# Attention output in column halves moved inside SBUF, and first weights converted in halves between the first products

## The chip, the core and the metric

The kernel runs on one core of a Trainium2 chip. The metric is the time of one execution in microseconds of device time; the median of three runs is taken.

## What is computed

A gated linear attention (a state of 48 x 48 numbers per head that decays and takes in one outer product per token) is followed by a SwiGLU feed-forward block. Everything is float32, but the three weight matrices arrive as float64.

```python
batch, n_heads, seq, head_dim = (4, 8, 768, 48)
for t in range(S):
    state = f[:, :, t, :, None] * state + np.einsum('bhd,bhe->bhde', k[:, :, t], v[:, :, t])
    y[:, :, t] = np.einsum('bhd,bhde->bhe', q[:, :, t], state)      # f = sigmoid(f_logit)
x = y.transpose(0, 2, 1, 3).reshape(B * S, H * D)                   # 3072 tokens x 384
g = x @ w_gate; silu = g / (1 + exp(-g)); val = x @ w_val           # d_ff = 1536
out = (silu * val) @ w_out
```

## The kernel before, in words

The 768 steps are cut into six chunks of 128 tokens. A unit is one batch of one chunk; the order is chunk 0 with its four batches, then chunk 1, and so on. While the feed-forward block of chunk c runs for its 512 tokens, the attention of chunk c + 1 is dealt in between (`take_turns`, L1001, with four steps a unit from `attention_steps`, L618). The general path at the head of the file runs only if a gate underflows; it does not in these runs.

**Attention of a unit** (`attention`, L504). Scans of the forget gate give factors for k and q; heads lie in pairs, one head in partitions 0 to 47, its neighbour in 64 to 111. Eight products of 48 rows give the scores (L563, `sc`), VectorE masks them into `A` (L565), and for all but the last chunk k is turned back by TensorE (L570, `kt`). Then comes the output `y`, feature by token, in one PSUM bank. Its 384 features are cut into quarters of 32: `place(n)` (L581) puts quarter n into partition group n mod 4. So that x comes out with 128 features in 128 partitions, quarters of 32 cross the borders of the heads of 48. From chunk 1 on, twelve products with `blocks` add the part of the state (L587): `blocks` holds the decayed state of a head pair as a block diagonal, filled by two ScalarE copies (L549). Sixteen products with v and `A` add the part inside the chunk (L596). One ScalarE copy (L599) moves the bank into `xT[c]`, the input of the feed-forward block. Eight products (L603, `dS`) and one VectorE sum (L607) update the state.

**Feed-forward.** Chunk 0 uses plain products (`mlp_plain`, L649): 12 gate and 12 val tiles of three products each, then the output (L679). Chunks 1 to 5 (`mlp_fifteen`, L778) form a 3 x 3 by 3 x 2 block product with 15 products instead of 18, four times over: sums of token blocks first (`token_sums`, L784, tile `xs`), then products into PSUM banks A, B, o and c (L825), copied aside by ScalarE (L830), added by VectorE (L717, L720). The output product takes seven products instead of eight (`down_seven`, L901; L923 and L977). The sums of weight blocks that this needs (`weight_sums`, L736) are made once, on VectorE, late in chunk 0 and in chunk 1.

**Weights.** They are fetched as float64 in 18 pieces of 768 KB and made float32: two ScalarE passes over a piece (`sizes`, L455 and L457) and four VectorE passes (`join`, L463 to L467). A gate or val piece covers two tiles of 128 columns. In `weights` (L1012) one fetch, one `sizes` and one `join` are dealt out after every pair of tiles.

**What sets the order.** Loads are issued by SyncE in one queue. Up to the mark near L1067 the order on TensorE, VectorE and ScalarE is that in which the code is written (`in_order`, L627); after that the Tile framework's scheduler places instructions, and each engine then works through its list in that order. Until L1067 the code walks through the attention of chunk 0 batch by batch, converts two pieces, and starts the products afterwards. The pool of attention tiles has one buffer for each tile.

Of the kernel before, what the change touches and what calls it, by code (L numbers as in the profile page):

```python
# [289 lines left out]
def short_path(ctx, tc, ident, least, judge, q, k, v, f_logit, moe_w_gate, moe_w_val, moe_w_out, out):  # L290
# [81 lines left out]
    decayed = const.tile([128, HP, D], FP32, tag="decayed", name="decayed")  # L372

    blocks = const.tile([128, HP, 2 * D], FP32, tag="blocks", name="blocks")
    nc.gpsimd.memset(blocks, 0.0)

    vs = [(const if i < NV // 2 else first_pool).tile([128, H, W], FP32, tag=f"v{i}", name=f"v{i}")
          for i in range(NV)]
    for t in vs:
        nc.gpsimd.memset(t[:, :, D:W], 0.0)  # L380

    w_both = const.tile([128, 2, KT, DFF], FP32, tag="w_both", name="w_both")
# [50 lines left out]
    def weight_piece(dst, src):  # L433

        if src.dtype == FP32:
            return (lambda: nc.sync.dma_start(out=dst, in_=src)), (lambda: None), (lambda: None)  # L440
        shape = list(dst.shape)
        kept = {}

        def fetch():
            kept["w"] = wst.tile(shape[:2] + [2 * shape[2]], I32, tag="w64", name="w64", bufs=3)
            nc.sync.dma_start(out=kept["w"], in_=src)

        def halves():
            words = kept["w"].rearrange("p a (n two) -> p a n two", two=2)
            return words[:, :, :, 0], words[:, :, :, 1]  # L450

        def sizes():
            lo, hi = halves()
            up = wst.tile(shape, I32, tag="up", name="up")
            nc.scalar.activation(up, lo.bitcast(U32), AF.Copy, scale=2.0 ** -29)  # L455
            top = wst.tile(shape, I32, tag="top", name="top")
            nc.scalar.activation(top.bitcast(FP32), hi.bitcast(FP32), AF.Abs)  # L457
            kept["up"], kept["top"] = up, top

        def join():  # L460
            lo, hi = halves()
            up, top = kept["up"], kept["top"]
            nc.vector.tensor_scalar(top.bitcast(FP32), top.bitcast(FP32), as_float(0x38000000), as_float(0x47F00000),  # L463
                                    op0=ALU.max, op1=ALU.min)
            nc.vector.tensor_scalar(top, top, 3, 0x3FFFFFFF, op0=ALU.logical_shift_left, op1=ALU.bitwise_and)
            nc.vector.scalar_tensor_tensor(top, hi, -(1 << 30), top, op0=ALU.bitwise_and, op1=ALU.bitwise_or)
            nc.vector.tensor_tensor(dst.bitcast(I32), top, up, ALU.add)  # L467

        return fetch, sizes, join
# [10 lines left out]
    NW = 256  # L480

    def add_piece(dst, src):
        for group, f in zip((fetches, sizes, joins), weight_piece(dst, src)):
            group.append(f)

    for j in range(0, DFF, NW):
        for dst, src in ((w_gate, moe_w_gate), (w_val, moe_w_val)):
            add_piece(dst[:, :, j:j + NW], in_rows(src)[:, :, per * j:per * (j + NW)])
    for i in range(NF // 2):
        both = slice(i, NF, NF // 2)  # L490
        add_piece(w_out[:, both, :], in_rows(moe_w_out)[:, both, :])
# [12 lines left out]
    def attention(u):  # L504
# [40 lines left out]
        if c:  # L545
            nc.vector.tensor_tensor(decayed, states[b], whole.broadcast_to((128, HP, D)), ALU.mult)
            for par in range(2):
                r = rows_of(par)
                nc.scalar.copy(blocks[r, :, par * D:(par + 1) * D], decayed[r])  # L549
# [4 lines left out]
        if 0 < c < SQUARES:  # L554
            load_after(u)
# [19 lines left out]
        if b == 0:  # L575
            xT[c] = ffn.tile([128, KT, TB], FP32, tag="xT", name="xT", bufs=2)


        y = bank("y")

        def place(n):  # L581
            return y[Q * (n % 4):Q * (n % 4) + Q, n // 4 * C:(n // 4 + 1) * C]

        per = 2 * D // Q
        if c:
            for n in range(DM // Q):
                nc.tensor.matmul(place(n), lhsT=blocks[:, n // per, n % per * Q:(n % per + 1) * Q], rhs=qT[:, n // per, :],  # L587
                                 start=n < 4, stop=False, skip_group_check=True)
        flat = v_.rearrange("t h e -> t (h e)")
        met = {n % 4 for n in range(DM // Q)} if c else set()  # L590
        for par in range(2):
            for n in range(DM // Q):
                h = 2 * (n // per) + par
                at = n * Q - h * D
                if -Q < at < D:
                    nc.tensor.matmul(place(n), lhsT=flat[:, W * h + at:W * h + at + Q], rhs=A[:, par, n // per, :],  # L596
                                     start=n % 4 not in met, stop=par == 1 or at + Q <= D, skip_group_check=True)
                    met.add(n % 4)
        nc.scalar.copy(xT[c][:, :, b * C:(b + 1) * C], y[:, 0:DM].rearrange("p (a t) -> p a t", t=C))  # L599
        if c < NCH - 1:  # L600
            p = bank("dS")
            for h in range(H):
                nc.tensor.matmul(p[W * (h % 2):W * (h % 2) + W, (h // 2) * D:(h // 2 + 1) * D],  # L603
                                 lhsT=kt[:, h, :], rhs=v_[:, h, 0:D], start=True, stop=True)
            dS = p[:, 0:HP * D].rearrange("p (a d) -> p a d", d=D)
            if c:
                nc.vector.tensor_tensor(states[b], decayed, dS, ALU.add)  # L607
            else:
                nc.scalar.copy(states[b], dS)
# [39 lines left out]
    def mlp_plain(c):  # L649
        h = {}  # L650

        def product(w, j, name):
            p = fps.tile([128, 512], FP32, tag="m", name=name)[:, 0:TB]
            for i in range(KT):
                nc.tensor.matmul(p, lhsT=w[:, i, j * 128:(j + 1) * 128], rhs=xT[c][:, i, :],  # L655
                                 start=(i == 0), stop=(i == KT - 1))
            return p

        def part(j):
            if j % NP not in h:  # L660
                h[j % NP] = hidden_tile()
            k = 2 * (j // NP)
            return h[j % NP][:, k:k + 2, :].rearrange("p a t -> p (a t)")

        def gate(j):
            p = product(w_gate, j, "gate")
            nc.scalar.activation(part(j), p, AF.Silu)

        def val(j):
            p = product(w_val, j, "val")  # L670
            nc.vector.tensor_tensor(part(j), part(j), p, ALU.mult)

        return ([lambda j=j, f=f: f(j) for i in range(0, NF, 2) for f in (gate, val) for j in (i, i + 1)],
                downs_abreast(c, h))
# [50 lines left out]
    extra = sums_pool.tile([128, 6, 2, NG], FP32, tag="extra", name="extra")  # L725

    def every_second(t, odd):

        return t.rearrange("p g (n two r) -> p g n two r", two=2, r=128)[:, :, :, odd, :]

    def weight_parts():
        w = {(i, k): w_both[:, :, k, i * NG:(i + 1) * NG] for i in range(KT) for k in range(KT)}
        e = [extra[:, n] for n in range(6)]
        return w, e

    def weight_sums(odd):  # L736

        w, e = weight_parts()
        w = {n: every_second(t, odd) for n, t in w.items()}
        e = [every_second(t, odd) for t in e]  # L740
# [37 lines left out]
    def mlp_fifteen(c):  # L778
# [32 lines left out]
        def triple(j):  # L811
            cols = slice(j * 128, (j + 1) * 128)
# [6 lines left out]
            def product(r):  # L819
                name, a, b = PRODUCTS[r]  # L820
                fresh = name == "o" or name not in p
                if fresh:
                    p[name] = both(name)
                for n in range(2):
                    nc.tensor.matmul(p[name][:, n, :], lhsT=weights_of[a][:, n, cols], rhs=tokens[b],  # L825
                                     start=fresh and n == 0, stop=True, skip_group_check=True)
# [208 lines left out]
    def load_ahead(u):  # L1035

        if u + NRAW < B:
            load(u + NRAW, "fkq")
            load(u + 1, "v")
        elif u + 1 < B:  # L1040
            load(u + 1, "v")
        if u + 1 < B:
            fetches.pop(0)()
        if u + NRAW >= B:
            load(u + NRAW)
# [19 lines left out]
    sizes.pop(0)()  # L1065
    joins.pop(0)()
    in_order(mark, (mybir.EngineType.PE, mybir.EngineType.DVE, mybir.EngineType.Activation))  # L1067


    for c in range(NCH):  # L1070
        if c == 0:
            hidden, last = mlp_plain(c)

            hidden = [f for i in range(NF) for f in hidden[2 * i:2 * i + 2] + [weights]]
            for i in range(len(joins) - NF):
                last.insert(3 * i, weights)
# [8 lines left out]
        take_turns(pieces, attention_steps(c + 1) if c + 1 < NCH else [], 2 if c else 8)  # L1085
# [85 lines left out]
```

## Time and profile before

| what | value |
|---|---|
| median of 3 runs | 632.69 us (630.79 to 632.91) |
| profiled execution | 630.66 us, span 628.9 us, granted TensorE clock 1.00 |
| TensorE busy | 611.1 us, 97% of the span |
| VectorE, ScalarE busy | 497.9 us (79%), 297.4 us (47%) |
| DMA | 48.00 MB in all, mean 76 GB/s, 237 GB/s at most in a slice |

A float32 product shows as two LDWEIGHTS records (`PEld`) and two MATMUL records (`PE`). The ends of matmuls are modelled and overlap, so durations of neighbouring groups are compared by their starts. In brackets behind an instruction stands how long its engine was idle before it, and what ended that.

### The profile page before, as it was taken

The page shows a single profiled execution, that of the slowest core. Times are in us where ns is not written, and L with a number is a line of the kernel's source. Part 1 is how long each engine was busy: PE and PEld are TensorE (multiplying, and loading weights), DVE is VectorE, ACT ScalarE, POOL GpSimd, SP SyncE. Part 2 cuts the span into 40 slices and gives each one's busy share as a digit, 9 for nine tenths or more (in the row PEclk, how much of TensorE's full clock was granted, in tenths as well). Part 3 has the DMA queues.
Part 4 walks back from the last instruction along what each step waited for, and adds up shares of the span by engine and source line. Part 5 has one row for each costly group of instructions (what it writes and reads, how often), then busy time and mean ns, then how long its engine had stood idle before and what let it go on. Part 6 is the DMA issues. An engine that isn't in the chain of part 4 may idle for free.

```text
span 628.9 us, 11292 instructions
## 1 busy us (share of the span) xinstructions
PE 611.1 (97%) x4420; PEld 494.2 (79%) x4420; DVE 497.9 (79%) x941; ACT 297.4 (47%) x546; POOL 3.2 (1%) x22
## 2 busy tenths in 40 slices
PE   7899999999999999999999999999999999999996
PEld 4744555666877899888889888889988889988896
DVE  7887889968999997589897479987678994357641
ACT  2463657214667812667631556650365540166600
POOL 1000000000000000000000000000000000000000
PEclk9999999999999999999999999999999999999999
DMA  9997465024222204122213213322301200100001
GB/s 152 237 223 236 146 177 163 3 67 134 62 67 76 73 21 123 38 66 71 69 39 89 75 27 74 83 60 69 97 27 39 64 1 1 52 1 2 0 1 55
DMA packets 87517, 48.00 MB, mean 76 GB/s; under 512 B 53664, under 2 KB 81312, under 8 KB 87456
## 3 DMA queue, kind: packets, MB, share of 16 engines
q1 hardware_dynamic: 84144, 42.68, 28.6%
q10 hardware_dynamic: 3312, 4.52, 2.0%
q8 instruction: 36, 0.59, 0.4%
q14 instruction: 25, 0.20, 0.1%
HBM read 42.47 MB, written 4.72 MB: 75 GB/s over the span
## 4 chain that ended last, share of the span: by engine, by line
PE 80%; DVE 10%; DMA 4%; ACT 4%; issue 1%; SPq 0%; ACTq 0%; DVEq 0%
PE o L923 17%; PE A L825 13%; PE B L825 11%; PE o L679 5%; PE gate L655 5%; PE val L655 5%; PE o L825 4%; PE c L825 4%; PE sc L563 3%; PE o L977 3%; PE y L596 2%; PE y L587 2%; DVE c L720 2%; PE kt L570 1%; DVE h L842 1%
## 5 line engine op out<-in xcount | busy, mean ns | idle before, releaser
L923 PE MATMUL o<-w_out,h 128*128 128x192 f32 x360 | 62.5, 330 | 1.2 <-ACT c L940 0.7
L825 PE MATMUL A<-xs,w_both 128*128 128x256 f32 x240 | 62.0, 380 | 0.0
L923 PEld LDWEIGHTS o<-w_out,h 128*128 128x128 f32 x360 | 58.2, 190 | 3.0 <-ACT c L940 1.5
L717 DVE TENSOR_TENSOR c<-c,aside 128x512 f32<-128x512 f32 x60 | 41.7, 695 | 21.3 <-ACT aside L830 20.5
L830 ACT COPY c<-A 128x512 f32<-128x512 f32 x40 | 23.4, 586 | 61.7 <-PE A L825 61.6
L830 ACT COPY aside<-A 128x512 f32<-128x512 f32 x60 | 35.2, 586 | 32.3 <-PE A L825 32.2
L825 PEld LDWEIGHTS A<-xs,w_both 128*128 128x128 f32 x240 | 45.1, 190 | 6.2
L842 DVE TENSOR_TENSOR h<-h,c 128x256 f32<-128x256 f32 x100 | 41.8, 426 | 7.6 <-ACT h L841 7.6
L720 DVE TENSOR_TENSOR c<-c,aside 128x512 f32<-128x512 f32 x60 | 41.7, 696 | 2.1 <-ACT aside L830 1.8
L841 ACT ACTIVATE h<-c 128x256 f32<-128x256 f32 x100 | 41.8, 421 | 2.4 <-DVE c L717 1.2
L825 PE MATMUL A<-xs,extra 128*128 128x256 f32 x160 | 41.3, 380 | 1.6 <-ACT c L830 0.9
L825 PE MATMUL B<-xs,w_both 128*128 128x256 f32 x160 | 41.9, 384 | 0.2
L825 PE MATMUL B<-xT,extra 128*128 128x256 f32 x160 | 41.6, 382 | 0.0
L825 PE MATMUL c<-xT,w_both 128*128 128x256 f32 x160 | 41.3, 380 | 0.0
L923 PE MATMUL o<-ws,h 128*128 128x192 f32 x240 | 41.0, 327 | 0.0
L830 ACT COPY aside<-B 128x512 f32<-128x512 f32 x60 | 35.0, 584 | 9.9 <-PE B L825 9.6
L923 PEld LDWEIGHTS o<-ws,h 128*128 128x128 f32 x240 | 39.0, 190 | 0.2
L720 DVE TENSOR_TENSOR c<-o,c 128x512 f32<-128x512 f32 x40 | 28.1, 703 | 13.2 <-PE o L825 12.7
L563 PEld LDWEIGHTS sc<-qT,kT 48*128 48x128 f32 x384 | 25.7, 187 | 12.9 <-issue 9.4
L825 PEld LDWEIGHTS A<-xs,extra 128*128 128x128 f32 x160 | 30.2, 190 | 6.5 <-ACT c L830 1.3
L599 ACT COPY xT<-y 128x384 f32<-128x384 f32 x24 | 11.5, 477 | 49.8 <-PE y L596 49.8
L565 DVE TENSOR_TENSOR A<-sc,causal 128x512 f32<-128x512 f32 x48 | 31.1, 688 | 3.9 <-PE sc L563 3.9
(127 smaller groups left out, 1197.1 us busy)
## 6 DMA issues: line engine op xcount, KB each, us to landing
fsquares<-in_f_logit_dram SPq DMA_DIRECT2D x64, 96.0 KB, 2.3
ksquares<-in_k_dram SPq DMA_DIRECT2D x64, 96.0 KB, 2.3
qsquares<-in_q_dram SPq DMA_DIRECT2D x64, 96.0 KB, 2.4
v<-in_v_dram SPq DMA_DIRECT2D x24, 192.0 KB, 3.7
w<-in_moe_w_gate_dram SPq DMA_DIRECT2D x6, 768.0 KB, 6.5
w<-in_moe_w_val_dram SPq DMA_DIRECT2D x6, 768.0 KB, 5.9
w<-in_moe_w_out_dram SPq DMA_DIRECT2D x6, 768.0 KB, 4.5
out_dram<-ob ACTq DMA_DIRECT2D x23, 192.0 KB, 1.9
```

Source lines behind the costliest of these rows:

```text
L563: nc.tensor.matmul(sc[par][:, a * C:(a + 1) * C], lhsT=kT[r, a, :], rhs=qT[r, a, :], start=True, stop=True)
L565: nc.vector.tensor_tensor(A[:, par], sc[par].rearrange("p (a t) -> p a t", t=C), causal.unsqueeze(1).broadcast_to((128, HP, C)), ALU.mult)
L655: nc.tensor.matmul(p, lhsT=w[:, i, j * 128:(j + 1) * 128], rhs=xT[c][:, i, :], start=(i == 0), stop=(i == KT - 1))
L679: nc.tensor.matmul(p, lhsT=h[n // 2][:, n % 2 * 2 + b // 2, b % 2 * C:(b % 2 + 1) * C], rhs=w_out[:, j, :], start=(n == 0), stop=(n == NF ...
L717: nc.vector.tensor_tensor(dst, a, b, ALU.add)
L720: nc.vector.tensor_tensor(dst, a, b, ALU.subtract)
L825: nc.tensor.matmul(p[name][:, n, :], lhsT=weights_of[a][:, n, cols], rhs=tokens[b], start=fresh and n == 0, stop=True, skip_group_check=True)
L830: nc.scalar.copy(t, p[name])
L841: nc.scalar.activation(dst, src[:, 0, :], AF.Silu)
L842: nc.vector.tensor_tensor(dst, dst, src[:, 1, :], ALU.mult)
L923: nc.tensor.matmul(p[:, n, :], lhsT=lhsTs[j][:, n * C:(n + 1) * C], rhs=rhs[:, j, :], start=first and j == 0 and n == 0, stop=j == NP - 1, ...
L977: nc.tensor.matmul(p3[:, n, :], lhsT=h[j][:, 2, n * C:(n + 1) * C], rhs=b22[:, j, :], start=n == 0 and j == 0, stop=j == NP - 1, skip_grou ...
```

## The change

It has three parts.

1. **Output in column halves.** Chunk 0 keeps the quarters of 32 columns (there is no state part yet). From chunk 1 on a head's 48 features, padded to 64, go to one half of the partitions, in two PSUM banks, one for each head of a pair: eight products with the decayed state (48 rows, 64 columns) and eight with v (128 rows, 64 columns). `blocks` and its two copies go; `decayed` gets padding columns that stay zero. Two ScalarE copies bring the banks to a tile `yT`, and ten DMA transfers from SBUF to SBUF, issued by SyncE, put the pieces of the heads (48, 32 or 16 partitions by 128 tokens) into their partitions of `xT[c]`.
2. **First weights in halves.** The pieces of the first two gate and the first two val tiles are converted in two halves each, in the order gate 0, val 0, gate 1, val 1, and the first products follow the conversions: gate 0, val 0, gate 1, val 1. The four products and the first two attention steps of chunk 1 now stand in the part whose order is written out. A fourth buffer holds fetched pieces, and the piece of val tiles 2 and 3 is fetched before the inputs of unit 5.
3. **Layout of the weights.** `w_both` holds the columns by tiles of 128 (`[128, 2, NF, KT, 128]`), so that a half is one run. One VectorE pass of a `join` becomes two over half the elements where a piece has two tiles.

```diff
-    w_both = const.tile([128, 2, KT, DFF], FP32, tag="w_both", name="w_both")
+    w_both = const.tile([128, 2, NF, KT, 128], FP32, tag="w_both", name="w_both")
...
-            kept["w"] = wst.tile(shape[:2] + [2 * shape[2]], I32, tag="w64", name="w64", bufs=3)
+            kept["w"] = wst.tile([128, a, 2 * b * n], I32, tag="w64", name="w64", bufs=4)
...
-            nc.vector.scalar_tensor_tensor(top, hi, -(1 << 30), top, op0=ALU.bitwise_and, op1=ALU.bitwise_or)
+            for i in range(b // parts):
+                nc.vector.scalar_tensor_tensor(top[:, i], hi[:, i], -(1 << 30), top[:, i], op0=ALU.bitwise_and,
+                                               op1=ALU.bitwise_or)
...
-            for par in range(2):
-                r = rows_of(par)
-                nc.scalar.copy(blocks[r, :, par * D:(par + 1) * D], decayed[r])
...
         if c:
-            for n in range(DM // Q):
-                nc.tensor.matmul(place(n), lhsT=blocks[:, n // per, n % per * Q:(n % per + 1) * Q], rhs=qT[:, n // per, :],
-                                 start=n < 4, stop=False, skip_group_check=True)
...
+            y = [bank("y") for _ in range(2)]
+            def place(a, par):
+                return y[par][W * (a % 2):W * (a % 2) + W, a // 2 * C:(a // 2 + 1) * C]
+            for a in range(HP):
+                for par in range(2):
+                    r = rows_of(par)
+                    nc.tensor.matmul(place(a, par), lhsT=decayed[r, a, :], rhs=qT[r, a, :],
+                                     start=a < 2, stop=False, skip_group_check=True)
+            for par in range(2):
+                for a in range(HP):
+                    nc.tensor.matmul(place(a, par), lhsT=v_[:, 2 * a + par, :], rhs=A[:, par, a, :],
+                                     start=False, stop=a >= HP - 2, skip_group_check=True)
+            yT = att.tile([128, 2, HP // 2 * C], FP32, tag="x", name="yT")
+            for par in range(2):
+                nc.scalar.copy(yT[:, par, :], y[par][:, 0:HP // 2 * C])
+            for h in range(H):
+                a, par = h // 2, h % 2
+                f = h * D
+                while f < (h + 1) * D:
+                    n = min((h + 1) * D, (f // 128 + 1) * 128) - f
+                    r = W * (a % 2) + f - h * D
+                    nc.sync.dma_start(out=xT[c][f % 128:f % 128 + n, f // 128, b * C:(b + 1) * C],
+                                      in_=yT[r:r + n, par, a // 2 * C:(a // 2 + 1) * C])
+                    f += n
...
     run(B - 1, 4)
-    sizes.pop(0)()
-    joins.pop(0)()
+    hidden, last = mlp_plain(0)
+    steps = attention_steps(1)
+    for _ in range(2):
+        sizes.pop(0)()
+        joins.pop(0)()
+    load(B + 1, "v")
+    for _ in range(2):
+        sizes.pop(0)()
+    hidden[0]()
+    joins.pop(0)()
+    steps.pop(0)()
+    joins.pop(0)()
+    hidden[1]()
+    weights()
+    hidden[2]()
+    steps.pop(0)()
     in_order(mark, (mybir.EngineType.PE, mybir.EngineType.DVE, mybir.EngineType.Activation))
```

## The prediction

> **What bounds the kernel now.** I read the page first, then busy time by stage, then the order of time around the places that the change touches.
>
> ```profile
> span 628.9 us, 11292 instructions
> PE 611.1 (97%) x4420; PEld 494.2 (79%) x4420; DVE 497.9 (79%) x941; ACT 297.4 (47%) x546; POOL 3.2 (1%) x22
> DMA  9997465024222204122213213322301200100001
> ```
>
> TensorE is busy nearly all the time; only the first eighth loads the DMA engines heavily. Busy time by stage (start; chunk 0; chunk 1; chunk 2):
>
> ```profile
> core 0: us, PE busy (x) PEld busy (x) DVE busy (x) ACT busy (x) POOL busy (x), PEclk, DMA share, GB/s
> 0.00:33.00 33.00, 26.45 (x341) 19.32 (x342) 27.42 (x49) 12.75 (x23) 2.91 (x19) 1.00 1.15 194
> 33.00:147.00 114.00, 114.00 (x649) 62.34 (x648) 95.94 (x161) 51.35 (x74) 0.24 (x3) 1.00 0.53 140
> 147.00:248.00 101.00, 96.86 (x765) 83.65 (x764) 98.34 (x184) 55.27 (x103) 0.00 (x0) 1.00 0.30 77
> 248.00:348.00 100.00, 99.18 (x777) 86.03 (x776) 80.97 (x158) 54.73 (x100) 0.00 (x0) 1.00 0.25 64
> ```
>
> After 33 us TensorE has no gap in chunk 0; in chunk 1 VectorE, at 98 of 101 us, is as full as TensorE. So a saving counts only where it shortens TensorE's work or the 33 us before the first product; in chunk 1 time that VectorE loses counts too. Scores and output of one unit in order of time on TensorE:
>
> ```profile
> 286.22 1.16 PE L563 MATMUL sc<-qT,kT 48*128 48x128 f32 x16
> 287.31 0.66 PE L570 MATMUL kt<-idf,kT 128*128 128x128 f32 x4
> ...
> 292.21 0.86 PE L587 MATMUL y<-qT,blocks 128*32 128x128 f32 x24
> 292.89 1.07 PE L596 MATMUL y<-A,v 128*32 128x128 f32 x32
> 293.90 0.67 PE L603 MATMUL dS<-v,kt 128*64 128x48 f32 x16
> 294.50 1.13 PE L825 MATMUL B<-xs,w_both 128*128 128x256 f32 x4
> ```
>
> The 24 records of the state part take 0.68 us from start to start: four run abreast, six rounds of 0.11 us. The next 32 are eight rounds, 0.88, and 0.13 more until `dS`, whose shape differs. `sc`, with two row halves abreast, has eight rounds in 1.09 us with its switch. The start of the products:
>
> ```profile
> 30.87 0.63 PE L513 MATMUL fTp<-idf,fraw 128*128 128x128 f32 x4 [0.36 <-DMA fraw<-in_f_logit_dram]
> 31.65 0.66 PE L513 MATMUL kTp<-idf,kraw 128*128 128x128 f32 x4 [0.15 <-DMA kraw<-in_k_dram]
> 32.76 0.63 PE L513 MATMUL qTp<-idf,qraw 128*128 128x128 f32 x4 [0.45 <-DMA qraw<-in_q_dram]
> 33.22 5.32 PE L655 MATMUL gate<-xT,w_both 128*128 128x512 f32 x12
> ```
>
> TensorE waits for the inputs of unit 4, though `xT` is complete at 30.46.
>
> **What the Trainium skill says.** "TensorEngine Tiling (Array Packing)", Key Properties: different tiles of the array run in parallel, and a change of tiling mode drains it. The trace agrees: rounds of four and of two, and 0.13 us at the switch. The same page, Gotcha 1: row tiles must write to different PSUM banks, hence two banks now, as `sc` has. "DMA: Bandwidth & Descriptors", Anatomy of one DMA: a semaphore wait is served on the issuing sequencer, before the transfer; so a transfer that waits for `yT` holds up the loads behind it. "TensorE: Matmul & The Clock Gate", on the array's sub-arrays: ScalarE and VectorE are strict FIFO; so a sum that waits for `xT` holds up every later VectorE instruction.
>
> **The change part by part.**
>
> *TensorE, output.* The twelve products with `blocks` become eight of 48 x 64. Two row halves by two column halves let four run abreast: four rounds instead of six. No row shows this tiling; bounds are four rounds (0.44) and, if only two run abreast, eight (0.88). I take four, because rows and columns each show it alone. The v part stays at eight rounds (16 records, two abreast). The switch moves: one between state part and v part, none before `dS`, which has the v part's shape. Balance: two rounds, 0.22 us a unit, in 16 units; in the last chunk's four, which have no `dS`, one switch is added: 0.22 - 0.13 = 0.09. The scheduled order breaks attention groups apart more often in chunks 1 and 4 (some five more pieces) and less often in chunk 2 (two fewer). A break costs two switches, some 0.3 us. Sum: chunk 0 stage -0.9; chunk 1 -0.9 + 1.0; chunk 2 -0.9 - 0.6; chunk 3 -0.9; chunk 4 -0.4 + 0.3.
>
> *ScalarE.* 40 copies of 348 ns go, 20 of 477 ns become 40 of half a bank (nearest row 421 ns, 256 elements): 23.4 us become 16.8. ScalarE is half idle, and waits of TensorE for it sum to some 4 us; I count nothing.
>
> *SyncE and xT.* 200 transfers of at most 24 KB. Issue: 0.34 us (an output's issue) to 0.43 (a square's, 1.73 us for four); landing 1.9 to 2.3 us. So `xT` is complete 0.85 + 3.4 to 4.3 + 2 = 6.3 to 7.2 us after the last product of `y`, against 0.5 before. Who waits: the token sums on VectorE, and behind them the evacuations of the output product. At the border of chunks 2 and 3 `y` ends at 337.8; `xT` at 344.8, ten sums at 0.335 and three evacuations make 349.5; TensorE wants the last of the first sums at 351.05. Hidden, with 1.5 us to spare. At the border of chunks 0 and 1 `y` ends at 133.3, `xT` comes at 140.3. VectorE has independent weight sums until 138.3, so it stands 2 us, and finishes the token sums at 144 instead of 141.6; several semaphores to wait for cost some more. Later VectorE is idle for 1.1 us before 151.43 and twice 0.25, which absorbs most; the rest, 0.8 us, comes out where L923 waits for VectorE's `h` at 221.12. The loads behind the transfers are needed a unit later: nothing. `yT` has one buffer, refilled 15 us later at the earliest: nothing.
>
> *Start.* Half a piece costs VectorE some 1.5 us instead of 3.0; `A` ends at 29.2, so gate 0 can start at 30.7, 2.5 us earlier. But 1.35 us of that was the work of the transposes of unit 4, which only move behind it: gain 1.1 us. Against it: the scan of unit 4 now stands behind the conversion of val tiles 2 and 3 and part of the next piece, whose transfer lands near 44.6 (ScalarE waited for it until 44.61). With 1.8 us of ScalarE and some 4 us of VectorE behind it, qT is ready near 50.6, and TensorE reaches `sc` at 49.5: it stands 1.1 us. I count -0.2.
>
> *Conversion in two passes of half size*: 12 extra passes, 0.06 us each on VectorE, beside TensorE's full 114 us: nothing. Layout: the products read as many rows as before: nothing.
>
> Sum: -0.2 - 0.9 + 0.8 (chunk 1: breaks and saving cancel, VectorE's delay stays) - 1.5 - 0.9 - 0.1 = -2.8; for the borders I add 0.3. 632.7 - 2.5 = 630.2 us.
>
> **Rivals.** *A clear gain* (chance 0.26): nothing of the transfers is seen, the start keeps its 1.1 us, ScalarE's relief takes 0.6 us of waits: 632.7 - 4.1 (0.22 x 16 + 0.09 x 4, with 0.2 of breaks) - 1.1 - 0.6, about 626.9. For it: TensorE's own work really shrinks, and 97% of the span is TensorE. Against: VectorE is full in chunk 1. *The transfers come too late* (0.18, slower): with other loads in the queue and eight transfers under way at a time, `xT` lands 10 us after `y`; VectorE then stands at all five borders, TensorE 1.5 to 2 us behind each, chunk 1 3 us: 632.7 - 3.5 + 8 = 637. For it: SyncE's squares at 0.43 us stand in the same queue. Against: 1.5 us to spare. *The small tiles do not run four abreast* (0.08, slower): eight rounds, 0.44 us x 20 more than forecast: 639. The forecast has 0.48.
>
> **How the numbers follow.** The likeliest case gives 630.2. A spread of 2 us (the three runs differ by that) puts 0.2 of its 0.48 below 629.5. With the rival's 0.24: faster 0.43. The two slow cases give 0.22 above 635.9; the rest is no change. From 625.8 to 637.0 holds 8 in 10.
>
> **What would show it.** Right: the state part at four rounds, 0.46 us between starts, and `y` to `dS` 1.47 us instead of 1.69; gate 0 near 30.7 with a wait at the first `sc` near 50; VectorE waiting about 2 us for the DMA of `xT` near 138, and no TensorE wait at later borders. Wrong: state-part records in pairs; issues of the transfers above 0.5 us, or sums that stand at every border; a longer stall near 50.

## The result, and the profile after

The changed kernel took 636.23 us (median of 4, 634.45 to 636.77) against 631.96 us of the kernel before beside it: ratio 1.0064, 95% interval 1.0034 to 1.0093. It is slower by some 4 us, where 2.5 us less was forecast. The time lies inside the range given, on the wrong side.

From the page of the profiled execution (634.45 us), the span, the busy times and the granted TensorE clock in 40 slices:

```profile
span 632.7 us, 10670 instructions
PE 610.4 (96%) x3940; PEld 492.4 (78%) x3940; DVE 501.3 (79%) x959; ACT 289.6 (46%) x530; POOL 2.9 (0%) x22
PEclk9999999999998999999999999999999999999999
```

TensorE has 480 records fewer and is busy for 0.7 us less, in a span that is 3.8 us longer. One slice has a lower clock; in the page of the kernel before every slice has 9. Busy time by stage (start; chunk 0; chunk 1; chunk 2):

```profile
core 0: us, PE busy (x) PEld busy (x) DVE busy (x) ACT busy (x) POOL busy (x), PEclk, DMA share, GB/s
0.00:31.00 31.00, 24.89 (x331) 18.22 (x331) 25.77 (x48) 10.27 (x20) 2.64 (x19) 1.00 1.15 193
31.00:147.00 116.00, 113.99 (x561) 62.80 (x562) 96.56 (x173) 55.26 (x77) 0.24 (x3) 1.00 0.54 146
147.00:251.60 104.60, 99.28 (x670) 84.91 (x669) 100.72 (x189) 54.48 (x99) 0.00 (x0) 0.98 0.30 77
251.60:350.00 98.40, 97.95 (x682) 85.30 (x682) 81.27 (x157) 48.64 (x93) 0.00 (x0) 1.00 0.30 78
```

The first product starts 2 us earlier, and chunk 0 takes 2 us more, so nothing is left of the start. Chunk 1 grows by 3.4 us and has a mean clock of 0.98; chunk 2 shrinks by 1.7 us. The output of one unit in order of time on TensorE (start, duration, line, tiles, count):

```profile
296.10 0.67 PE L600 MATMUL y<-qT,decayed 48*64 48x128 f32 x16
296.70 1.09 PE L604 MATMUL y<-A,v 128*64 128x128 f32 x16
297.62 0.62 PE L637 MATMUL dS<-v,kt 128*64 128x48 f32 x16
298.18 1.13 PE L855 MATMUL B<-xs,w_both 128*128 128x256 f32 x4
```

From `y` to `dS` it is 1.52 us (1.69 before), from `y` to the next product 2.08 us (2.29 before). The single records of the state part start in four groups of four. So TensorE does save 0.21 us a unit; in the four units of the last chunk it is 0.06 (1.62 us from `y` to the next product, 1.68 before). The start:

```profile
31.20 2.81 PE L689 MATMUL gate<-xT,w_both 128*128 128x512 f32 x6 [0.68 <-DVE w_both L473]
...
48.04 1.88 PE L689 MATMUL val<-xT,w_both 128*128 128x512 f32 x4
51.73 1.16 PE L574 MATMUL sc<-qT,kT 48*128 48x128 f32 x16 [1.81 <-DVE qT L562]
```

And what TensorE waited for in the whole execution (total us, times, longest), two lines of its waits, first changed, then before:

```profile
PE sc L574 <- DVE qT L562: 5.7, 5, 1.8
PE o L1007 <- DVE ob L752: 3.5, 4, 1.5
```

```profile
PE sc L563 <- DVE qT L553: 1.9, 3, 0.8
PE o L977 <- DVE ob L717: 0.4, 1, 0.4
```

`ob` holds the output on its way out: its instructions on VectorE are the evacuations of the output product. Together the two waits are 6.9 us more: more than the 3.6 us that the shorter output saves in 16 units at 0.21 and four at 0.06.

For what follows, the time from the first product of a chunk to that of the next (the last one to the end), in us from the traces. Three of them hold stretches in which TensorE ran at half its clock, each 1.7 us of the time given: one in chunk 1 of the changed kernel and of the one with evacuations first, one each in chunks 0 and 1 of the one without transfers. The section on the clock comes to them.

| kernel | first product | chunk 0 | 1 | 2 | 3 | 4 | 5 |
|---|---|---|---|---|---|---|---|
| before | 33.22 | 113.66 | 101.23 | 100.12 | 99.07 | 93.56 | 88.03 |
| changed | 31.20 | 115.78 | 104.62 | 98.39 | 98.95 | 94.22 | 89.57 |
| halves of the output alone | 33.41 | 112.51 | 102.99 | 98.38 | 97.65 | 94.59 | 89.16 |
| start and layout alone | 31.17 | 116.04 | 101.27 | 100.10 | 99.09 | 93.56 | 87.96 |
| order held, no transfers | 31.21 | 117.46 | 104.52 | 98.46 | 97.54 | 93.70 | 87.86 |
| order held, evacuations first | 31.21 | 115.78 | 104.60 | 97.80 | 97.48 | 93.87 | 88.03 |
| order mended, third | 31.10 | 113.90 | 103.07 | 97.80 | 97.55 | 94.06 | 88.18 |

### The profile page after: what moved, and what is told of

It is laid out like the page before. It is cut to its first block, busy times and chain, and to the rows that moved or that the text cites. A ratio compares the mean times of both kernels' runs of the same rounds, so it can differ in the third digit from the quotient of the medians.

```text
span 632.7 us, 10670 instructions
## 1 busy us (share of the span) xinstructions
PE 610.4 (96%) x3940; PEld 492.4 (78%) x3940; DVE 501.3 (79%) x959; ACT 289.6 (46%) x530; POOL 2.9 (0%) x22
## 4 chain that ended last, share of the span: by engine, by line
PE 70%; DVE 14%; ACT 4%; SPq 4%; DMA 4%; issue 3%; DVEq 0%; ACTq 0%
PE A L855 13%; PE o L953 13%; PE B L855 11%; PE o L855 4%; PE c L855 4%; PE val L689 4%; PE sc L574 4%; SPq L615 4%; PE gate L689 3%; PE o L714 3%; PE y L604 3%; PE o L1007 2%; PE y L600 2%; DMA xT<-yT 2%; PE kt L581 1%
## 5 line engine op out<-in xcount | busy, mean ns | idle before, releaser
L574 PE MATMUL sc<-qT,kT 48*128 48x128 f32 x384 | 30.3, 287 | 5.7 <-DVE qT L562 5.7
L855 PEld LDWEIGHTS B<-xT,extra 128*128 128x128 f32 x160 | 30.0, 191 | 6.6 <-ACT aside L860 2.4
L855 PEld LDWEIGHTS c<-xT,w_both 128*128 128x128 f32 x160 | 30.8, 193 | 4.2
```

The source lines that it names most:

```text
L574: nc.tensor.matmul(sc[par][:, a * C:(a + 1) * C], lhsT=kT[r, a, :], rhs=qT[r, a, :], start=True, stop=True)
```

## Which part of the change costs the time

**Theory T:** the transfers make `xT` late; the token sums stand, and what is behind them on VectorE and SyncE comes late. **Rival S:** the new order of the start costs more than it gains. First each part alone. The diffs from here on are shortened.

The kernel before with the output's part of the diff, and nothing of the start or the layout:

```diff
-        y = bank("y")
+            y = [bank("y") for _ in range(2)]
...
-        nc.scalar.copy(xT[c][:, :, b * C:(b + 1) * C], y[:, 0:DM].rearrange("p (a t) -> p a t", t=C))
+                    nc.sync.dma_start(out=xT[c][f % 128:f % 128 + n, f // 128, b * C:(b + 1) * C],
+                                      in_=yT[r:r + n, par, a // 2 * C:(a // 2 + 1) * C])
```

> The kernel before with only the output in halves and the SBUF transfers; first weights and layout as before. Theory T (the transfers make xT late, so token sums stand and the evacuations and loads behind them come late): nearly all of the 4 us loss is here, 635 to 637 us. Rival S (the new order of the start costs more than it gains): without it the halves keep their 0.2 us a unit, 628 to 630 us.

The other way round, the changed kernel with the output of before:

```diff
-            y = [bank("y") for _ in range(2)]
+            y = bank("y")
...
-                    nc.sync.dma_start(out=xT[c][f % 128:f % 128 + n, f // 128, b * C:(b + 1) * C],
+        nc.scalar.copy(xT[c][:, :, b * C:(b + 1) * C], y[:, 0:DM].rearrange("p (a t) -> p a t", t=C))
```

> The changed kernel with the output put back to quarters and one ScalarE copy; conversion of the first weights in halves, their order and the layout stay. Theory T: the same as before within 1 us, 631 to 633 us, because the earlier first product (2 us) is lost again at the first score product. Rival S: 635 to 637 us.

Halves alone: 631.63 us, ratio 1.0001 (0.9989 to 1.0013). Start alone: 631.40 us, 0.9998 (0.9985 to 1.0011). Neither theory had this: each part by itself costs nothing, and only both together cost 0.6%. S falls, since the start alone is free: its first product is 2.05 us earlier and its chunk 0 is 2.38 us longer. T is half right: with the halves alone the chunks differ from before by -1.15, +1.76, -1.74, -1.42, +1.03 and +1.13 us. The output saves what it should in chunks 0, 2 and 3, and chunks 1, 4 and 5 take it back. That the two together cost more than either shows in their waits: for the evacuation TensorE waits 2.3 us with the halves alone and 3.5 in the changed kernel, at the first score product 1.2 us with the start alone and 1.8 in the changed kernel. Much of the rest is clock, as will be seen.

Then the transfers. One kernel leaves them out (ScalarE copies the two banks straight into `xT`, where the features then stand in wrong rows), one issues half of them from ScalarE:

```diff
-            yT = att.tile([128, 2, HP // 2 * C], FP32, tag="x", name="yT")
+            to = xT[c][:, :, b * C:(b + 1) * C]
...
-                nc.scalar.copy(yT[:, par, :], y[par][:, 0:HP // 2 * C])
+            nc.scalar.copy(to[:, 0:2, :], y[0][:, 0:HP // 2 * C].rearrange("p (a t) -> p a t", t=C))
+            nc.scalar.copy(to[:, 1:3, :], y[1][:, 0:HP // 2 * C].rearrange("p (a t) -> p a t", t=C))
```

> The changed kernel with the 200 transfers left out: ScalarE copies the two banks of y straight into xT, 256 columns each, so the features of xT stand in the wrong rows and a third of them is overwritten. Theory T: the waits behind the late xT (3.8 us before the last output products, 3.4 us in chunk 1) go and the shorter y stays, 628 to 630 us. Rival S: 635 us. Rival W (the small tiles save nothing on TensorE): 632 us.

```diff
-                    nc.sync.dma_start(out=xT[c][f % 128:f % 128 + n, f // 128, b * C:(b + 1) * C],
+                    (nc.scalar if h % 2 else nc.sync).dma_start(out=xT[c][f % 128:f % 128 + n, f // 128, b * C:(b + 1) * C],
```

> The changed kernel with the transfers of the odd heads issued from ScalarE instead of SyncE, so that ten issues of 0.59 us become two lists of five and xT is complete some 3 us earlier. Theory T: about half of the loss is regained, 633 to 634.5 us. Rival S: 636 us. Rival C (ScalarE's own work is delayed by the issues): above 636 us.

Without transfers: 630.53 us, 0.9979 (0.9968 to 0.9989), less of a gain than T said. With two queues: 635.36 us, 1.0067 (1.0048 to 1.0087), nothing regained. There TensorE waits only 1.2 us before L1007 instead of 3.5, but 4.6 us for ScalarE's copies `aside` instead of 1.2: an issue holds ScalarE's queue for 0.60 us (median of 100), and the copies stand behind it. That is rival C of this expectation.

These four kernels share one weakness: the scheduler places instructions anew after every edit. Without the transfers it puts a score product elsewhere, and TensorE stands near 3 us for it in chunk 1 (2.80 by the profile), and the mean clock is 0.994. So the next kernels hold the order.

## The same with the order held

Each engine's list is kept as the changed kernel's program has it; `ORDER` holds the numbers of the instructions as the code writes them, in the order of that program.

```diff
+    for name, order in ORDER.items():
+        base = [ins for ins in traced if ins.engine == kinds[name] and type(ins).__name__ not in LEFT]
+        keep_order([base[n] for n in order])
```

> The changed kernel with every engine's order held as the scheduler gave it and nothing else changed: it shows that holding the order is itself free, and how its clock varies over many executions. 635 to 637 us, mean clock 0.994 to 0.995.

It took 634.94 us, 1.0054 (1.0041 to 1.0067): like the changed kernel, so holding the order is free. Its mean clock was 0.997 here (five executions), 0.9945 in the four of the changed kernel, which fits its being 1.3 us faster.

**Without transfers, same order** (the edit is that of the kernel without transfers above).

> The changed kernel with every engine's order of instructions held as the scheduler gave it, but without the 200 transfers: ScalarE's two copies go straight into xT (features in wrong rows, a third overwritten). Theory T (late xT): the waits before the last output products (3.8 us) and most of the 3.4 us of chunk 1 go, so 6 us less than the changed kernel, 629 to 631 us. Rival O (the order that the scheduler chose is worse, whatever the transfers do): 634 to 636 us.

630.82 us, 0.9996 (0.9984 to 1.0008): T's number, so the transfers cost some 4 us in this order. But the table shows where: chunks 3, 4 and 5 are 1.4, 0.5 and 1.7 us shorter than in the changed kernel, chunk 1 is not (chunk 0 is longer for a reason that comes under the clock). The time in chunk 1 is not the transfers' doing. (Without them SyncE also fetches its loads earlier; that did not shorten chunk 1 either.)

**The evacuation ahead of the sums.** At a border the program has the first half of the last output product evacuated before TensorE writes the second half into the same bank. In the changed kernel at the border of chunks 2 and 3, VectorE in order of time:

```profile
349.33 0.43 DVE L758 SCALAR_TENSOR_TENSOR xs<-xT 128x256 f32<-128x256 f32 x1 [1.22 <-DMA xT<-yT]
...
350.34 0.55 DVE L752 TENSOR_TENSOR ob<-c,o 128x384 f32<-128x384 f32 x1
350.80 0.42 DVE L755 TENSOR_TENSOR xs<-xT 128x256 f32<-128x256 f32 x1
351.14 0.75 DVE L752 TENSOR_TENSOR xT<-xT 128x256 f32<-128x256 f32 x2
351.81 0.35 DVE L752 TENSOR_TENSOR ob<-c,o 128x192 f32<-128x192 f32 x1
```

and TensorE:

```profile
348.03 2.11 PE L1007 MATMUL o<-w_out,h 128*128 128x192 f32 x12
349.98 1.03 PE L855 MATMUL A<-xs,w_both 128*128 128x256 f32 x4
352.21 2.22 PE L1007 MATMUL o<-w_out,h 128*128 128x192 f32 x12 [1.20 <-DVE ob L752]
```

The first half was ready near 350.2, but its evacuation (351.81) stands behind sums that stood for `xT`. TensorE could have gone on at 350.85, when the four products `A` were through. The experiment moves that one instruction ahead, at four borders:

```diff
+    for position, target in ((410, 408), (569, 565), (726, 725), (864, 860)):
+        ORDER["DVE"].insert(target, ORDER["DVE"].pop(position))
```

> The changed kernel, same order but for four VectorE instructions: the evacuation of the first half of the last output product is put ahead of the token sums that still stand before it (one to four sums). Theory T: TensorE no longer waits before the second half (3.8 us in four borders in the trace); 3 to 4 us less than the changed kernel, 632 to 633 us. Rival (TensorE then waits for the sums instead): 635 to 636 us.

631.34 us, 1.0003 (0.9992 to 1.0013): four VectorE instructions moved by one to four places give back 3.6 us against the held order, all but some tenths of the loss. It is not the clock: executions with a mean clock of 0.996 or 0.997 took 630.5 to 631.7 us here and 634.3 to 635.2 in the held order. At the same border, on VectorE (both evacuations now follow the seventh sum) and on TensorE:

```profile
349.72 0.81 DVE L752 TENSOR_TENSOR ob<-c,o 128x192 f32<-128x192 f32 x2
```

```profile
349.39 1.03 PE L855 MATMUL A<-xs,w_both 128*128 128x256 f32 x4
350.25 2.11 PE L1007 MATMUL o<-w_out,h 128*128 128x192 f32 x12
```

The second half follows at once, though VectorE still stood 1.19 us for `xT`. So the late `xT` itself was bearable. What it did was to push an evacuation that TensorE needed. Little else of the transfers is left: at a mean clock of 0.998 or more this kernel took 628.9 and 629.0 us (two executions), the one without transfers 629.2 to 629.3 (three).

**Loads ahead of transfers.** At the first border the loads of f for unit 8 now stood behind ten transfers: issued at 140.26 instead of 134.09.

```diff
+    first = SP.index(first_transfer_of_unit_7)
+    SP[first:first] = [SP.pop(SP.index(n)) for n in loads_of_f_for_unit_8]
```

(The names stand for numbers in SyncE's list.)

> The changed kernel, same order but for SyncE at the first border: the four loads of f for unit 8 are issued ahead of the ten transfers of unit 7, not behind them. Theory T: VectorE gets gates 3 to 4 us earlier, xT 1.9 us later; the stalls at the score products of chunk 1 (1.97 and 0.77 us) shrink: 1.5 to 3 us less than the changed kernel, 633 to 634.5 us. Rival (what holds chunk 1 is the late xT itself): no change or up to 1.5 us more, 636 to 637.5 us.

635.43 us, 1.0066 (1.0052 to 1.0080): no change, though the loads were issued at 136.25, ahead of the transfers. Neither these loads nor, by the run without transfers, the late `xT` hold up chunk 1.

**How much is the number of transfers.** The same bytes in twice as many:

```diff
-                    nc.sync.dma_start(out=xT[c][f % 128:f % 128 + n, f // 128, b * C:(b + 1) * C],
-                                      in_=yT[r:r + n, par, a // 2 * C:(a // 2 + 1) * C])
+                    for at in (0, C // 2):
+                        nc.sync.dma_start(out=xT[c][f % 128:f % 128 + n, f // 128, b * C + at:b * C + at + C // 2],
+                                          in_=yT[r:r + n, par, a // 2 * C + at:a // 2 * C + at + C // 2])
```

> The changed kernel, same order, with each of the ten transfers of a unit cut into two of 64 columns: the same bytes, twenty issues. Theory T (the time of the issues on SyncE sets when xT is complete, 0.59 us each): xT comes 6 us later at five borders; 3 to 6 us of it show at each of four, 648 to 660 us. Rival (the transfers themselves, not their number, set it): 636 to 640 us.

709.0 us, 1.1230 (1.1216 to 1.1245). The direction is T's, the size far above it. A transfer of half the bytes takes the same 0.59 us to issue, so it is their number that sets when `xT` comes. TensorE waits 29.4 us before L1007 (8.5 at most) and 16.6 us for ScalarE's copies, and the mean clock is 0.953: ten stretches at half rate, 68 us in all, in which TensorE was busy for 44 us, so that they cost some 22 us. That second term was not in the expectation.

## The clock

Why is the changed kernel's clock lower? In its chunk 1, TensorE in order of time:

```profile
197.13 1.16 PE L574 MATMUL sc<-qT,kT 48*128 48x128 f32 x16 [1.80 <-DVE qT L562]
...
198.78 1.92 PE L855 MATMUL c<-xT,w_both 128*128 128x256 f32 x4
200.49 1.80 PE L855 MATMUL A<-xs,w_both 128*128 128x256 f32 x4
202.13 1.03 PE L855 MATMUL B<-xT,extra 128*128 128x256 f32 x4
```

The stall before `sc` is 2.0 us long when the records ahead of it are counted at their rate; the profile's 1.80 starts from their modelled end. (The stalls named in this section are counted by rate.) Four records take 1.71 and 1.64 us from start to start here, and 0.87 us elsewhere: half the rate. The trace's record of the granted clock has the half from 198.64 to 202.06, for 3.41 us. Halving is what the Trainium skill says in "TensorE: Matmul & The Clock Gate", Part 1: the clock gate passes half the pulses after an idle window of about 3.4 us, and all of them after a busy window of that length; the window runs freely, not from the kernel's start. The length of the slow stretch agrees, and so does the raster: the stretches of one trace begin whole multiples of 3.413 us apart (in the one without transfers in held order at 53.22 and 199.99, 43 of them). The idle time does not: 2.0 us were enough here, and not in every execution (the same stall at 51.73 was followed by the full clock in this execution, and by half of it in the profile of the kernel without transfers in held order, which is why chunk 0 is longer there). A stall may fall differently into the windows each time; that this decides was not shown.

Under work without a gap, 3.41 us at half rate cost 1.7 us. The executions of one kernel show it as steps: without transfers in held order, three with a mean clock of 1.000 took 629.2 to 629.3 us, seven with 0.996 or 0.997 took 630.7 to 631.1, four with 0.993 or 0.994 took 632.5 to 632.9. Of 51 executions of the kernel before, 29 with 0.999 or 1.000 took 630.9 us on average, 17 with 0.996 or 0.997 took 632.8.

**Theory C:** stalls of about 2 us lower the clock, and that is part of the loss. To tell, the two long stalls (units 4 and 10) are filled with products whose result is overwritten, everything else in the same order:

```diff
         sc = [bank("sc") for _ in range(2)]
+        for _ in range({4: 7, 10: 7}.get(u, 0)):
+            nc.tensor.matmul(sc[0], lhsT=ones.bitcast(mybir.dt.bfloat16)[:, 0:128],
+                             rhs=ones.bitcast(mybir.dt.bfloat16)[:, 0:512], start=True, stop=True)
```

> The changed kernel, same order, with seven 512-column bf16 products of zeros and ones put ahead of the score products of units 4 and 10, where TensorE stands 2 us each. They change no other engine. Theory C (after a stall of 2 us TensorE runs for some us at a lower clock, so part of the loss is clock): mean clock from 0.994 to 0.998 and 1.5 to 2.5 us less than the changed kernel, 633.5 to 634.5 us. Theory T alone: no change, 636 us, or some tenths more.

632.98 us, 1.0032 (1.0020 to 1.0044), mean clock 0.9985 over 11 executions. TensorE's work grew, and some 2 us are gone (2.0 by the ratio of the changed kernel, 1.4 by that of the held order). At the same place:

```profile
195.07 1.67 PE L570 MATMUL sc<-ones 128*128 128x512 bf16 x7
197.05 1.16 PE L574 MATMUL sc<-qT,kT 48*128 48x128 f32 x16 [0.30 <-DVE qT L562]
198.14 0.66 PE L581 MATMUL kt<-idf,kT 128*128 128x128 f32 x4
198.63 1.03 PE L855 MATMUL c<-xT,w_both 128*128 128x256 f32 x4
199.50 0.81 PE L855 MATMUL A<-xs,w_both 128*128 128x256 f32 x3
```

The score product starts when it did, and the products after it keep 0.87 us for four. So C is shown for these two stalls. The one slow stretch in this trace, from 544.36 to 547.78, stands elsewhere, behind a wait of 2.3 us for an evacuation at the last border:

```profile
541.02 0.60 PE L855 MATMUL A<-xs,w_both 128*128 128x256 f32 x2
543.77 3.67 PE L1007 MATMUL o<-w_out,h 128*128 128x192 f32 x12 [2.15 <-DVE ob L752]
```

The eight executions with a mean clock of at least 0.998 took 632.7 us on average, 1.8 more than the kernel before at full clock. By that estimate some 2 of the 4.3 us lost are waits, less what the output saves, and the rest is clock. Over the kernels (stalls after the first 5 us; slow stretches ahead of the last product):

| kernel | TensorE stalls near 2 us or longer, in its trace | slow stretches, in its trace | mean clock (executions) |
|---|---|---|---|
| before | none (1.6 at most) | none | 0.998 (51) |
| start alone | none (1.6 at most) | none | 0.998 (14) |
| halves alone | one | none | 0.997 (22) |
| changed | two | one | 0.9945 (4) |
| order held | two | one | 0.997 (5) |
| evacuations first | two | one | 0.996 (22) |
| stalls filled | the two filled, one of 2.3 left | one | 0.9985 (11) |
| order mended, third | none (1.4 at most) | none | 0.998 (6) |

The mean clock is taken over the whole span, and a stretch at half rate behind the last product costs nothing: in the trace of the third mended order it begins at 622.76, the last product at 620.06, and it alone takes 0.002 off the mean. Nor is it a strict rule that a stall lowers the clock: 2.8 us in the first mended order below were followed by the full clock, 2.9 us in the same order with the evacuations first by half of it. And the kernel before had a third of its executions at 0.996 or 0.997; what lowers the clock there stays open.

## Mending the order

The long stalls themselves are VectorE's order: qT of units 4 and 10 stands behind work that could wait. The scans of unit 4 go ahead of a weight piece, into a gap where VectorE waited for ScalarE; four products `h` (VectorE's, element by element) go behind qT of unit 10. The lists below show the moves by name; the edit moves numbers in `ORDER`.

```diff
 VectorE, start:    h (L705)
+                   tails, least, start, start, head (L541 to L561)
                    top, top, top, top, w_both (L467 to L473)
-                   tails, ..., head
 VectorE, chunk 1:  c, c, c (L752, L755)
+                   head, qT (L561, L562)
                    h, h, h, h (L872)
-                   head, qT
```

> The changed kernel, same order but for VectorE in two places: the scans of unit 4 are put ahead of the conversion of a weight piece (they fit where VectorE waited for ScalarE), and four products h of chunk 1 are put behind qT of unit 10. The evacuations at the borders stay as they were. Theory C: both stalls of 2 us at score products shrink below 0.5 us and the clock after them does not fall: 2 x 1.5 us of stall and 2 us of clock, 631 to 632.5 us. Rival (TensorE waits elsewhere for what was moved back): 634.5 to 636 us, with the clock at 0.998.

> The changed kernel with the two VectorE moves of the run before and the evacuations ahead of the token sums; all other engines as the scheduler gave them. If theories T and C are both right their parts add: 636.2 less 4 to 4.9 (evacuations) less 4 to 5 (stalls and clock), 626.5 to 628.5 us, faster than the kernel before. If one of them only hides the other: 630 to 631 us.

633.11 us, 1.0033 (1.0023 to 1.0042), and with the evacuations first 630.18 us, 0.9984 (0.9970 to 0.9998). Half of it worked: the stall of unit 4 is gone and chunk 0 took 113.90 us instead of 115.78. In chunk 1 the wait moved: one of the four `h` frees the tile `c32`, ScalarE's next copy into it stood, and TensorE waited 2.6 us for that copy by the profile. So the second try leaves two of the four where they were, and puts qT of unit 11 forward as well; the third drops the latter.

```diff
 VectorE, chunk 1:  h, kT, c, h, c, c
+                   head, qT (L561, L562)
                    h, h (L872)
-                   head, qT
 VectorE, unit 11:
+                   qT, qT (L554, L562)        in the second try only
                    hs, state, hs, h
-                   qT, qT
```

> As the run with the order mended, but in chunk 1 only the two products h directly ahead of qT of unit 10 are put behind it (four of them held up ScalarE's copies, and TensorE stood 2.8 us for those), and qT of unit 11 is put ahead of two sums of h. If the stall in chunk 1 is the order's doing: 2.8 and 0.8 us of stall become about 1 us, and the clock after it does not fall, so 1.5 to 3 us less than the run before, 627 to 629 us, clearly faster than the kernel before (631.1 us). If VectorE simply has too much work there: TensorE waits as long elsewhere, 630 us.

> As the run before, without the move for unit 11, behind which TensorE stood 1.8 us for h before the output products. Order: the stall of 0.8 us at the score product of unit 11 comes back, the 1.8 us and the lower clock after them go; 1 to 2.5 us less, 626.5 to 628 us. Load: the same wait appears elsewhere, 629 us.

629.10 us, 0.9966 (0.9954 to 0.9978), with a wait of 1.8 us (2.0 by rate, and half the clock after it) that appeared for `h` before the output products; and without the move for unit 11 627.67 us, 0.9939 (0.9921 to 0.9957), mean clock 0.998. From the waits of TensorE in this last kernel:

```profile
PE sc L574 <- DVE qT L562: 4.0, 4, 1.3
```

The wait for qT is still there, but no single one is longer than 1.3 us, and no wait for the evacuation is left but 0.4 us at the end. With the same work on every engine as in the changed kernel, a dozen VectorE instructions at other places make it 7 to 8 us faster, and 0.6% faster than the kernel before. Chunk 1 is still 1.8 us longer than before. It is so in every kernel of the table with the halves, once 1.7 us is taken off for each slow stretch: 1.8 with the halves alone, 1.7 in the changed kernel, 1.6 without transfers. VectorE was busy for 100.7 of the 104.6 us there in the changed kernel, and each try at the order left a wait somewhere in it. What the 1.8 us are stays open.

## Why the prediction was wrong

- **State part four abreast, 0.22 us a unit: right.** Four rounds; 0.17 us less up to `dS`, 0.04 less from `dS` to the next product, and 0.06 in the last chunk's units (0.09 forecast).
- **Sum by stage: right where nothing waits.** Chunk 2 was to save 1.5 us and saved 1.7; with the halves alone chunk 0 saved 1.15 (0.9 forecast) and chunk 3 1.4 (0.9).
- **Start, -0.2: near in the sum, off in its terms.** First product at 31.2 (30.7 forecast), stall at the first `sc` 1.8 us (1.1), start alone +0.3 us in the trace up to the end of chunk 0, ratio 0.9998.
- **Issue of a transfer, 0.34 to 0.43 us: mis-sized.** It takes 0.59 us, as the median of the 200. Ten take 6 us, and where VectorE's sums stood for the last of `xT`, they got it 8 to 9.6 us after the last product of `y` (6.3 to 7.2 forecast). The 1.5 us to spare were gone by that alone.
- **"TensorE wants the last of the first sums at 351.05": the step that failed.** It named the wrong consumer. The third of "three evacuations" behind the ten sums was the one that TensorE wanted first, before the second half of the last output product. The trace of before has this pair too, and there VectorE stood ready for it:

```profile
348.43 0.35 DVE L717 TENSOR_TENSOR ob<-c,o 128x192 f32<-128x192 f32 x1 [1.40 <-PE o L977]
349.10 2.11 PE L977 MATMUL o<-w_out,h 128*128 128x192 f32 x12
```

TensorE wanted this evacuation done by 349.10. The prediction's own sum ended at 349.5, so that nothing was to spare even at its price for the transfers. At the four borders with this pair, moving that one instruction gives back 3.6 us.

- **The clock: in no step and in no rival.** The forecast had a stall of 1.1 us at the start and counted its length. Two stalls of 2 us cost up to 1.7 us each on top through the clock, some 2 us over the executions.
- **Chunk 1, +0.8 by VectorE: cause wrong, size too small.** It is +1.8 us with the halves alone and +3.4 in the changed kernel's trace, of which the slow stretch is 1.7. The late `xT` does not do it: removing the transfers and moving the loads left chunk 1 as it was. That the scheduler's new order on a full VectorE does it is argued, not shown.
- **Loads behind the transfers, nothing: right,** though they came 6.2 us later.
- The rival *transfers too late* (637 us) gave the time, by waits at the borders of the kind that happened; of its 8 us about half were there, and the clock filled the rest. That the sum came near 636 is luck.

## What to carry to other kernels

When a transfer replaces a copy, list what stands behind its first reader on that engine, and ask of each whether another engine waits for it sooner than for the reader; put those ahead. Price small transfers by their number and a measured issue time of the same kind (0.59 us here, for 8 KB as for 24), not by that of the nearest load. A wait of TensorE near 2 us may cost up to 1.7 us more in clock after it, so two of them are worth breaking up or filling. And when experiments change what a scheduler sees, hold the order, or each measures a new order as well.

## What was not expected of the hardware

A stall of 2.0 us was followed by 3.41 us at half the rate in part of the executions, on a raster of 3.413 us; but for the kernel with twice the transfers, whose stalls come close together, none up to 1.7 us was followed by it in a trace here. An issue from SyncE takes 0.59 us for SBUF to SBUF, at 24 KB and at 12 KB alike, and 0.60 from ScalarE. And a four-instruction change of order on VectorE weighs as much as 480 TensorE records: 3.6 us each.
